# Second layer's weights rebuilt from four fp32 sums on every pass, a wider spread of the gate's products, and another order of the two layers on TensorE

## The chip, the cores and the metric

The kernel runs on one core of one Trainium2 chip. The metric is device time in microseconds (us), the median of several runs. The profile is of one execution: its rows count from the start of the span, the time from the first to the last instruction.

## What is computed

Pooled attention, then two feed-forward parts over 2304 tokens of width 512. The last part is the one that the change touches:

```python
logits = x @ w_gate
logits = logits - logits.max()
P = np.exp(logits)
for _ in range(8):
    P /= P.sum(1, keepdims=True) + 1e-09
    P /= P.sum(0, keepdims=True) + 1e-09
    P *= N / E
out = np.zeros((N, D), dtype=np.float32)
for e in range(E):
    h = np.maximum(x @ w1[e], 0.0)
    ye = h @ w2[e]
    out += P[:, e:e + 1] * ye
```

Here N = 2304, D = 512, E = 8, and the hidden width of each expert is 1024.

## The kernel before

Every fp32 operand of a product is kept as a pair, a rounded high part and the low rest, and each product is three matmuls (high by high, high by low, low by high). `split` (L93) makes a pair: ScalarE copies to the high part (`whi`), VectorE or GpSimd subtracts it from the source to give the low part (`wlo`).

Up to about 533 us the kernel does the attention and the first feed-forward part. Then it goes over three pairs of token blocks (768 tokens each) and, inside each pair, over 16 units (8 experts by two halves of the hidden width). One unit of one pair is a **step**, 48 in all. In a step TensorE does the first layer of that unit and, woven into it, the second layer of the unit before.

The first layer (`first_layer`, L740) is a Strassen-like scheme of seven products P1, P5, P6, P2, P7, P3, P4, for two halves g = 0 and 1 of the unit: 14 products of six matmuls of 384 columns, called **a0 to a13** here (a0 to a6 for g = 0, a7 to a13 for g = 1). P1 goes to the PSUM bank `px`, ScalarE copies it to `py`, and P6 adds to that copy. P5 and later P3 use the one bank `pv`. The results leave the banks through ScalarE (relu) and VectorE.

In pair 0 the second layer is plain (`plain_layer`, L843): six groups **L** of 24 matmuls of 256 columns, with the four blocks of the second weight matrix. In pairs 1 and 2 it is Strassen-like as well (`strassen_layer`, L860): three row groups 0, 1, 2, each with four parts of 12, 12, 12 and 6 matmuls of 256 columns. The strings `PLAIN`, `SWAP` (the step between pairs 0 and 1) and `STRASSEN` write out the order of TensorE by hand: `a` is the next product of the first layer, `L` the next plain group, a digit the next part of that row group. The other engines' orders are made by a scheduler; each engine, and SP's DMA queue, works strictly in its order. What follows a product is hung on its slot with `put(places, todo)`.

The second layer's weights: in pair 0 `w2_pieces` (L617) loads the fp32 weights of a unit, splits the four blocks, forms four sums on GpSimd (P5, P6, P7, P4), splits these too, and writes seven pairs to DRAM (`w2c`, 14 DMAs of 256 KB a step). In pairs 1 and 2 `w2_cached` (L667) loads the seven pairs, 14 DMAs a step. The first layer's weights go the same way (`w1_pieces` L574, `w1c`, `w1_cached`), loaded seven slots ahead.

The gate (softmax and eight rounds of row and column scaling, the "halves") is hung on the slots of the first steps by the list `rest` (L969): one entry after each even slot.

Of the kernel before, what the change touches and what calls it, by code (L numbers as in the profile page):

```python
# [58 lines left out]
def fused_kernel(ctx: ExitStack, tc: tile.TileContext, qT, kT, vT, v0, wa1, wb1, wa2, wb2, wg, out):  # L59
# [459 lines left out]
    def gate_max():  # L519

        sk, lg = gate["sk"], gate["lg"]
        m1 = sk.tile([P, 1], F32, tag="m1", name="m1")
        nc.vector.tensor_reduce(out=m1, in_=lg, op=ALU.max, axis=AX.XY)
# [90 lines left out]
    def w2_pool(name):  # L614
        return wp if name in ("P1", "P5") else gate["wp2"]

    def w2_pieces(u):  # L617

        src, w = {}, {}

        def load(h):
            src[h] = xp.tile([P, 2, DM], F32, tag=("xh5", "xl5")[h], name="raw2")
            nc.sync.dma_start(out=src[h], in_=wb2[u, :, h])

        def b(h, d):
            return src[h - 1][:, :, (d - 1) * HD:d * HD]

        def flat(t):
            return t.rearrange("p (g n) -> p g n", g=2)

        def cut(what, pool, lo_engine):
            hi = pool.tile([P, FU], F32R, tag="w", name="vhi")
            lo = pool.tile([P, FU], F32R, tag="w", name="vlo")
            nc.scalar.activation(out=flat(hi), in_=what, func=AF.Copy)
            lo_engine.tensor_tensor(out=flat(lo), in0=what, in1=flat(hi).bitcast(F32), op=ALU.subtract)  # L635
            return hi, lo

        def keep(name, parts):
            for k, part in enumerate(parts):
                nc.sync.dma_start(out=w2c[u, ORDER.index(name), k], in_=part.bitcast(F32))  # L640

        def block(h, d):
            w[h - 1, d - 1] = cut(b(h, d), gate["wp2"], nc.gpsimd)
            name = {(1, 1): "P1", (2, 1): "P2", (2, 2): "P3"}.get((h, d))
            if name:
                keep(name, w[h - 1, d - 1])

        def tmp():
            return gate["tmp"].tile([P, 2, HD], F32, tag="s", name="t")

        def total(name):
            if name == "P5":
                src["t"] = combine(tmp(), b(1, 2), b(1, 1), ALU.subtract)
                what = src["t"]
            elif name == "P6":
                what = combine(src["t"], b(2, 2), src["t"], ALU.subtract)
            elif name == "P7":
                what = combine(tmp(), b(2, 2), b(1, 2), ALU.subtract)
            else:
                what = combine(src["t"], b(2, 1), src["t"], ALU.subtract)  # L660
            keep(name, cut(what, gate["wp2"], nc.vector))

# [452 lines left out]
```

## Time and profile before

| | us |
|---|---|
| median of 3 runs (lowest, highest) | 2041.63 (2041.26, 2043.84) |
| the profiled execution's own time | 2042.21 |
| its span | 2040.5 |
| TensorE busy in the span | 1966.0 |
| VectorE, ScalarE, GpSimd busy | 1380.9, 992.3, 770.8 |

A matmul is pipelined: in the timeline its modelled end lies after the start of the next, so the rate is read from one start to the next, and busy time is no measure of it. An idle time in square brackets is followed by what ended it. The granted clock is the share of TensorE's full clock, 1.00 being 2.4 GHz and 0.50 being 1.2 GHz.

### The profile page before, as it was taken

The numbers are of one execution on the slowest core, as the hardware profiler recorded it, in microseconds if no ns is written. First come the engines' busy times: TensorE is split into PE (matmuls) and PEld (weight loads), VectorE is DVE, ScalarE is ACT, GpSimd is POOL, SyncE is SP. The second block draws the span as 40 slices with busy tenths as digits, with TensorE's granted clock in tenths as the row PEclk, the third lists the DMA queues.
The fourth block names the chain that finished last, engine by engine and source line by source line (L and its number), as shares of the span: only waits on it lengthen the run. The fifth ranks groups of instructions, "written<-read, shape, count | busy, mean of one in ns | idle before, by whom it ended". The sixth has DMA issues, their size and how long they took to land.

```text
span 2040.5 us, 36395 instructions
## 1 busy us (share of the span) xinstructions
PE 1966.0 (96%) x13220; PEld 1917.3 (94%) x13220; DVE 1380.9 (68%) x2279; ACT 992.3 (49%) x2133; POOL 770.8 (38%) x646
## 2 busy tenths in 40 slices
PE   6799999999889999999999999999999999999999
PEld 4689899999889999999999999999998999999999
DVE  8988776655786555556565676667667666666766
ACT  5676566655544444434443444444445444444443
POOL 7755644433344545454532221222223222222212
PEclk8899999999989999999999999999999999999999
DMA  7433331212688988888896776677677777667763
GB/s 254 144 123 126 113 119 53 84 52 77 228 292 296 304 276 301 270 293 292 278 316 222 266 263 229 240 275 250 225 256 250 241 261 275 230 235 269 258 230 121
DMA packets 257458, 453.32 MB, mean 222 GB/s; under 512 B 25568, under 2 KB 86752, under 8 KB 257280
## 3 DMA queue, kind: packets, MB, share of 16 engines
q1 hardware_dynamic: 257280, 451.01, 64.5%
q8 instruction: 104, 1.70, 0.3%
q14 instruction: 74, 0.61, 0.1%
HBM read 317.21 MB, written 133.69 MB: 221 GB/s over the span
## 4 chain that ended last, share of the span: by engine, by line
PE 76%; DVE 6%; DMA 6%; POOL 4%; ACT 3%; issue 3%; SPq 0%; ACTq 0%; POOLq 0%; DVEq 0%
PE pc L869 13%; PE py L736 13%; PE qc L869 10%; PE po L852 8%; PE px L736 8%; PE pv L736 8%; DMA w2c<-vhi 2%; PE ph L138 2%; PE po L137 2%; PE po L139 2%; PE ph L139 2%; PE po L138 2%; PE ph L137 2%; POOL vlo L635 1%; POOL t L571 1%
## 5 line engine op out<-in xcount | busy, mean ns | idle before, releaser
L869 PE MATMUL pc<-wc,gh 128*128 128x256 f32 x1536 | 284.1, 280 | 0.0
L571 POOL TENSOR_TENSOR sf<-spare 128x384 f32<-128x384 f32 x64 | 65.7, 1027 | 509.9 <-DVE spare L800 509.9
L869 PEld LDWEIGHTS pc<-wc,gh 128*128 128x128 f32 x1536 | 241.1, 188 | 0.0
L736 PE MATMUL py<-xc,wc 128*128 128x384 f32 x1152 | 236.1, 340 | 0.9 <-DVE c L794 0.6
L869 PE MATMUL pc<-wc,gl 128*128 128x256 f32 x768 | 215.6, 281 | 0.0
L869 PE MATMUL qc<-wc,gh 128*128 128x256 f32 x1152 | 214.1, 280 | 1.5 <-DVE pc L888 1.5
L736 PEld LDWEIGHTS py<-xc,wc 128*128 128x128 f32 x1152 | 196.6, 189 | 7.4 <-ACT py L751 5.1
L783 DVE TENSOR_TENSOR gl<-sf,gh 128x384 fp32r<-128x384 f32 x256 | 183.8, 758 | 10.8 <-ACT gh L782 7.3
L869 PEld LDWEIGHTS qc<-wc,gh 128*128 128x128 f32 x1152 | 185.9, 188 | 2.0 <-DVE pc L888 1.8
L869 PE MATMUL qc<-wc,gl 128*128 128x256 f32 x576 | 161.7, 281 | 0.0
L571 POOL TENSOR_TENSOR sf<-sf 128x384 f32<-128x384 f32 x64 | 80.8, 1262 | 210.9 <-DVE gl L783 210.9
L736 PE MATMUL pv<-xc,wc 128*128 128x384 f32 x768 | 156.2, 338 | 3.8 <-DVE xc L716 2.0
L736 PE MATMUL px<-xc,wc 128*128 128x384 f32 x768 | 154.3, 335 | 0.0
L852 PE MATMUL po<-vlo,gh 128*128 128x256 f32 x768 | 153.1, 281 | 0.0
L852 PE MATMUL po<-vhi,gl 128*128 128x256 f32 x768 | 152.8, 281 | 0.0
L852 PE MATMUL po<-vhi,gh 128*128 128x256 f32 x768 | 152.6, 281 | 0.0
L782 ACT ACTIVATE gh<-sf 128x384 fp32r<-128x384 f32 x256 | 119.9, 517 | 52.5 <-POOL sf L571 32.8
L869 PEld LDWEIGHTS pc<-wc,gl 128*128 128x128 f32 x768 | 145.1, 189 | 0.2 <-DVE gl L783 0.2
L137 PE MATMUL ph<-xh,whi 128*128 128x384 f32 x384 | 131.3, 346 | 5.9 <-DVE r L389 5.9
L736 PEld LDWEIGHTS pv<-xc,wc 128*128 128x128 f32 x768 | 131.0, 189 | 4.6 <-DVE xc L716 2.2
L138 PE MATMUL ph<-xl,whi 128*128 128x384 f32 x384 | 131.5, 343 | 0.7 <-DVE xl L370 0.7
L138 PE MATMUL po<-gl,whi 128*128 128x384 f32 x384 | 129.5, 338 | 0.8 <-POOL gl L392 0.8
(203 smaller groups left out, 5136.1 us busy)
## 6 DMA issues: line engine op xcount, KB each, us to landing
wc<-w1c SPq DMA_DIRECT2D x448, 256.0 KB, 5.2
wc<-w2c SPq DMA_DIRECT2D x448, 256.0 KB, 5.4
w1c<-whi SPq DMA_DIRECT2D x112, 256.0 KB, 3.4
w1c<-wlo SPq DMA_DIRECT2D x112, 256.0 KB, 3.3
w2c<-vhi SPq DMA_DIRECT2D x112, 256.0 KB, 3.9
w2c<-vlo SPq DMA_DIRECT2D x112, 256.0 KB, 4.3
raw<-wa SPq DMA_DIRECT2D x48, 512.0 KB, 6.2
raw<-wb SPq DMA_DIRECT2D x48, 512.0 KB, 4.6
```

Of the source, the lines that this page charges most:

```text
L137: nc.tensor.matmul(out=ps, lhsT=lh, rhs=rh, start=(i == 0), stop=False)
L138: nc.tensor.matmul(out=ps, lhsT=lh, rhs=rl, start=False, stop=False)
L139: nc.tensor.matmul(out=ps, lhsT=ll, rhs=rh, start=False, stop=(i == n - 1))
L571: nc.gpsimd.tensor_tensor(out=out, in0=x, in1=y, op=op)
L635: lo_engine.tensor_tensor(out=flat(lo), in0=what, in1=flat(hi).bitcast(F32), op=ALU.subtract)
L736: nc.tensor.matmul(out=ps, lhsT=l[:, k], rhs=r[:, c, :], start=(start and c + n == 0), stop=(c + n == 3), skip_group_check=True)
L782: nc.scalar.activation(out=hi, in_=t, func=AF.Copy)
L783: nc.vector.tensor_tensor(out=lo, in0=t, in1=hi.bitcast(F32), op=ALU.subtract)
L852: nc.tensor.matmul(out=po[:, d * HD:(d + 1) * HD], lhsT=l[:, r], rhs=w[f % 2, d][k][:, (f // 2) * HD:(f // 2 + 1) * HD], start=(f + n + d ...
L869: nc.tensor.matmul(out=ps, lhsT=l[:, r], rhs=m[:, k], start=(start and g + n == 0), stop=(g + n == 3), skip_group_check=True)
```

## The change

Second layer's weights. `w2_sums` loads a unit's raw weights once more, forms the four sums with GpSimd and writes them unsplit to DRAM (`w2s`, 4 DMAs of 256 KB); these jobs run in steps 2 to 14 of pair 0. `w2_piece` loads one fp32 tile of 256 KB (a block of the input, or a sum) into one of four buffers `st` and splits it: four blocks a step in pair 0, seven pieces a step in pairs 1 and 2. P2, P4 and the blocks (2,1), (2,2) take their low part on VectorE, all others on GpSimd. The write-out of 14 split tiles and the loads of 14 are gone.

Gate. `logits` and the maximum are cut in two, and `rest` names the slots: the last logits after a1 and a3, the maximum after a6, the exponential and first row scaling after a8, one half after a12 of step 0, then one after every odd slot of step 1.

Order. `PLAIN`, `STRASSEN` and the places of several `put` lists are new. The first unit's `w1_pieces` moves into the last task of the part before, the low parts of the first two units of the first layer go to GpSimd, and the inputs of pair 1 are prepared from slots 2 and 7 on.

```diff
+    w2s = dram.tile([NU, 4, P, FU], F32, name="w2s")
...
-            parts = split(what, nc.vector)
+            parts = split(what, nc.gpsimd if u < 2 else nc.vector)
...
+    W2RAW = {"P1": (1, 1), "P2": (2, 1), "P3": (2, 2)}
+    W2SUM = ("P5", "P6", "P7", "P4")
+
+    def w2_piece(u, name, w):
+
+        src = st.tile([P, FU], F32, tag="st", name="st")
+        if name in W2SUM:
+            nc.sync.dma_start(out=src, in_=w2s[u, W2SUM.index(name)])
+        else:
+            i, j = W2RAW.get(name, name)
+            nc.sync.dma_start(out=src, in_=wb2[u, :, i - 1, j - 1])
+        engine = nc.vector if name in ("P2", "P4") or name in BLOCKS[2:] else nc.gpsimd
+        w[name] = split(src, engine, wp if name == "P1" else gate["wp2"])
+
+    def w2_sums(u):
...
+        def total(k):
+            b = {(i, j): r[i - 1][:, j - 1, :] for i in (1, 2) for j in (1, 2)}
+            t, s = r[0][:, 2, :], r[1][:, 2, :]
+            out, x, y = ((t, b[1, 2], b[1, 1]), (s, b[2, 2], t), (b[1, 2], b[2, 2], b[1, 2]),
+                         (b[2, 1], b[2, 1], s))[k]
+            combine(out, x, y, ALU.subtract)
+            nc.sync.dma_start(out=w2s[u, k], in_=out)
...
+                    if f == 2 and j == GRP[1][1] and u == U1 - 1:
+                        w_op, w_load, w_todo = w1_pieces(0)
+                        run(w_load, 2)
...
-    gate["wp2"] = right(ctx, "wp2", 18, reuse_waits="tile")
+    gate["wp2"] = right(ctx, "wp2", 16, reuse_waits="tile")
+    st = right(ctx, "st", 4, reuse_waits="tile")
...
-    rest = [[lambda: logits(GRP[1][1])], [gate_max], [gate_exp, sinkhorn_rows], [], half, [], half]
-    rest += [half] * (SINKHORN_ITERS - 3) + [[sinkhorn_columns]]
+    rest = [{1: [late_logits], 3: [late_turn], 6: [max_turn], 8: [gate_exp, sinkhorn_rows], 12: half},
+            {2 * k + 1: half for k in range(SINKHORN_ITERS - 2)}]
+    rest[1][13] = half[:1]
...
-    GB = {"gl": 20, "gh": 16}
-    PLAIN = "aaLaaLaaLaaLaaLaaLaa"
+    GB = {"gl": 17, "gh": 17}
+    PLAIN = "aaLaaLaaLaaaLaaLaaLa"
     SWAP = "aaLaLLLLLsaaaaaaaaaaa"
-    STRASSEN = "aaa0a1a01a01a01a2aa2a2a2aa"
+    STRASSEN = "aa0a1a0a1a0a1a0a2a1a2a2a2a"
...
-                    put((0, 0), load)
-                    put((1, 3, 5, 7, 8, 9, 10, 11) if not last else (1, 2, 3, 4, 5, 6, 7, 8), todo)
-                    put(range(0, 14, 2), w_todo)
+                    put((2, 4, 6, 8), [lambda b=b, u=u, w=w2: w2_piece(u, b, w) for b in BLOCKS])
+                    put(range(5, 12), w_todo)
+                    if n > 1 and not last:
+                        for k in (0, 6)[:1 + (n > 11)]:
+                            put((k, k + 2, k + 3, k + 3, k + 4), w2_sums(jobs.pop(0)))
...
-                    put((6, 7, 8, 9, 10, 11, 12), [lambda m=m, u=u, w=w2: w2_cached(u, w, m) for m in ORDER])
+                    put(range(7, 14), [lambda m=m, u=u, w=w2: w2_piece(u, m, w) for m in ORDER])
...
-                    put((8, 8) if pair == 0 else (2, 2), x_load)
-                    put((10, 10, 11, 11, 12, 12, 13) if pair == 0 else range(7, 14), x_todo)
+                    put((2, 2), x_load)
+                    put(range(7, 14), x_todo)
```

**VectorE in step 0 of pair 0**, from the maximum's arrival (`nm`) to the first column sum (`cs`), which the gate's next product waits for. Before:

```order
L536 COPY nm<-pb 128x1
L725 SCALAR_TENSOR_TENSOR gl<-c_5757,gh 128x384
L543 TENSOR_REDUCE rw<-pr 128x18
L544 TENSOR_SCALAR rw<-rw 128x18
L545 RECIPROCAL rw<-rw 128x18
L725 SCALAR_TENSOR_TENSOR gl<-pv_5701,gh 128x384
L546 TENSOR_TENSOR pr<-pr,rw 128x144
L97 TENSOR_TENSOR wlo<-s,whi 128x512
L725 SCALAR_TENSOR_TENSOR gl<-py,gh 128x384
L548 TENSOR_REDUCE cs<-pr 128x8
```

With the change:

```order
L546 COPY nm<-pb 128x1
L738 TENSOR_TENSOR pv_5806<-py,s_5813 128x384
L553 TENSOR_REDUCE rw<-pr 128x18
L554 TENSOR_SCALAR rw<-rw 128x18
L555 RECIPROCAL rw<-rw 128x18
L556 TENSOR_TENSOR pr<-pr,rw 128x144
L707 SCALAR_TENSOR_TENSOR gl<-px_5790,gh 128x384
L558 TENSOR_REDUCE cs<-pr 128x8
```

The low part of a first-layer weight (L97) and two of the three `gl` rows have left this chain; one addition to `pv` came in.

**ScalarE in a step of pair 0**, up to P1's copy (`py`). `vhi` is the high part of a second-layer weight, `t` a sum just made, `whi<-raw` and `whi<-s` belong to the first layer, `gh` to its results, `st` is a fresh fp32 load. Before:

```order
L634 ACTIVATE vhi<-t 128x512
L724 ACTIVATE gh<-c_8549 128x384
L634 ACTIVATE vhi<-t 128x512
L724 ACTIVATE gh<-pv_8447 128x384
L724 ACTIVATE gh<-py 128x384
L634 ACTIVATE vhi<-t 128x512
L96 ACTIVATE whi<-raw 128x512
L751 ACTIVATE py<-px_8620 128x384
```

With the change:

```order
L706 ACTIVATE gh<-pv_9226 128x384
L96 ACTIVATE whi<-st 128x512
L96 ACTIVATE whi<-s 128x512
L96 ACTIVATE whi<-st 128x512 x2
L706 ACTIVATE gh<-py 128x384
L96 ACTIVATE whi<-st 128x512
L733 ACTIVATE py<-px_9398 128x384
```

The rows `vhi<-t`, whose tiles were also written out to `w2c`, are gone from ahead of `py`; the blocks' rows `whi<-st` stand there instead.

**ScalarE in the second half of a step of pair 2**, from P2's result (`spare`, after a10) to P1's copy of the next step. `c` is P7's result, `sf<-pv` P3's (it frees the bank `pv`), `sf<-py` P4's. Before:

```order
L802 ACTIVATE spare<-px_23205 128x384
L805 ACTIVATE gh<-px_23205 128x384
L802 ACTIVATE c_23315<-c_23315 128x384
L802 ACTIVATE sf<-pv_23237 128x384
L782 ACTIVATE gh<-spare 128x384
L782 ACTIVATE gh<-c_23315 128x384
L802 ACTIVATE sf<-py 128x384
L751 ACTIVATE py<-px_23385 128x384
```

With the change:

```order
L784 ACTIVATE spare<-px_23262 128x384
L787 ACTIVATE gh<-px_23262 128x384
L96 ACTIVATE whi<-st 128x512 x3
L784 ACTIVATE c_23380<-c_23380 128x384
L96 ACTIVATE whi<-st 128x512 x2
L784 ACTIVATE sf<-pv_23286 128x384
L764 ACTIVATE gh<-spare 128x384
L764 ACTIVATE gh<-c_23380 128x384
L96 ACTIVATE whi<-st 128x512
L784 ACTIVATE sf<-py 128x384
L733 ACTIVATE py<-px_23474 128x384
```

Six of the seven new splits (the seventh, P1's, stands further ahead) lie between these results: five ahead of `sf<-pv`, one ahead of `sf<-py`.

## Rows read from the trace of the kernel before

**Rows 1.** The page, busy time and share of the span of each engine.

```profile
PE 1966.0 (96%) x13220; PEld 1917.3 (94%) x13220; DVE 1380.9 (68%) x2279; ACT 992.3 (49%) x2133; POOL 770.8 (38%) x646
```

**Rows 2.** Stretch, us, busy PE PEld DVE ACT POOL, granted clock, DMA share, GB/s.

```profile
533.38:601.00 67.62, 52.42 (x308) 49.23 (x307) 52.55 (x111) 27.29 (x52) 32.43 (x24) 0.87 0.84 292
601.00:1062.00 461.00, 449.06 (x3231) 444.59 (x3230) 270.23 (x416) 197.51 (x376) 230.15 (x165) 1.00 0.86 290
...
1105.00:1530.00 425.00, 425.00 (x3030) 422.80 (x3029) 286.26 (x460) 192.32 (x458) 97.39 (x86) 1.00 0.70 245
1530.00:1560.00 30.00, 26.07 (x167) 24.83 (x166) 24.65 (x32) 17.55 (x36) 13.98 (x8) 0.94 0.71 236
```

**Rows 3.** TensorE's waits, 533 to 601 us: total, times, longest.

```profile
PE pc L555 <- DVE cs L548: 10.6, 4, 7.8
PE pv L736 <- DVE gl L725: 1.8, 1, 1.8
PE pm L525 <- DVE m L523: 1.6, 1, 1.6
```

**Rows 4.** Timeline of TensorE in that stretch: start, duration, then the instruction.

```profile
555.24 0.52 PE L736 MATMUL px<-xl,whi 128*128 128x384 f32 x1
555.56 0.52 PE L736 MATMUL px<-xh,wlo 128*128 128x384 f32 x1
...
570.49 0.59 PE L555 MATMUL pc<-cs,ones 128*128 128x8 f32 x2 [7.81 <-DVE cs L548]
```

**Rows 5.** Timeline of VectorE, then of GpSimd, 543 to 553 us.

```profile
544.29 0.15 DVE L536 COPY nm<-pb 128x1 f32<-128x1 f32 x1
...
549.79 1.77 DVE L97 TENSOR_TENSOR wlo<-s,whi 128x512 fp32r<-128x512 f32 x1
...
551.95 0.40 DVE L548 TENSOR_REDUCE cs<-pr 128x8 f32<-128x144 f32 x1
...
548.43 4.26 POOL L635 TENSOR_TENSOR vlo<-raw,vhi 128x512 fp32r<-128x512 f32 x3
```

**Rows 6.** Waits of TensorE and ScalarE, 601 to 1062 us, and ScalarE's timeline.

```profile
PE py L736 <- ACT py L751: 10.3, 11, 1.7
...
ACT vhi L634 <- DMA w2c<-vhi: 76.6, 34, 6.8
...
691.33 0.63 ACT L634 ACTIVATE vhi<-t 128x512 fp32r<-128x512 f32 x1 [4.22 <-DMA w2c<-vhi]
...
692.38 0.47 ACT L751 ACTIVATE py<-px 128x384 f32<-128x384 f32 x1
```

**Rows 7.** Timeline of TensorE in one step of pair 2.

```profile
1815.67 1.21 PE L736 MATMUL pv<-xc,wc 128*128 128x384 f32 x6
1816.71 1.32 PE L736 MATMUL py<-xc,wc 128*128 128x384 f32 x6
1817.87 0.40 PE L869 MATMUL pc<-wc,gh 128*128 128x256 f32 x2
...
1819.31 1.21 PE L736 MATMUL px<-xc,wc 128*128 128x384 f32 x6
```

**Rows 8.** Groups by line: busy us, mean ns, idle before and its releasers.

```profile
L96 ACT ACTIVATE whi<-raw 128x512 fp32r<-128x512 f32 x136 | 82.9, 625 | 27.9 <-DMA raw<-wb1f 8.7 <-DMA raw<-wa1f 7.0 <-PE po L139 6.8
...
L635 POOL TENSOR_TENSOR vlo<-raw,vhi 128x512 fp32r<-128x512 f32 x64 | 91.2, 1440 | 70.9 <-PE po L852 40.9 <-DMA w2c<-vlo 15.2 <-ACT vhi L634 9.1
...
L97 DVE TENSOR_TENSOR wlo<-raw,whi 128x512 fp32r<-128x512 f32 x80 | 60.5, 757 | 3.5 <-PE px L736 2.0 <-PE pv L736 0.2
```

**Rows 9.** DMA issues: KB each, median us to landing.

```profile
wc<-w2c SPq DMA_DIRECT2D x448, 256.0 KB, 5.4
...
raw<-wb1f SPq DMA_DIRECT2D x14, 512.0 KB, 3.6
out<-acc SPq DMA_DIRECT2D x18, 256.0 KB, 2.0
```

**Rows 10.** TensorE's longest wait, 1530 to 1560 us.

```profile
PE pv L736 <- ACT sf L802: 1.8, 1, 1.8
```

More of the change, by code (lines that the diff above doesn't have):

```diff
@@ L485, in open_gate @@
         gc = right(ctx, "gc", 1, reuse_waits="tile")
-        gate["sk"] = right(ctx, "sk", 2, reuse_waits="tile")
+        gate["sk"] = right(ctx, "sk", 1, reuse_waits="tile")
         gate["tmp"] = right(ctx, "tmp", 3, reuse_waits="tile")
@@ L504, in logits, with logits_first @@
     def logits(j):
-        sk = gate["sk"]
+        lt = logits_first(j)
+        logits_turn(j, lt)
+    def logits_first(j):
         ps = gate["ps"][0].tile([P, NB], F32, tag=gate["ps"][1], name="pl")
@@ L517, in logits, with max_first, max_turn @@
         nc.vector.tensor_copy(out=gate["lg"][:, j * TPB:(j + 1) * TPB, :], in_=pq)
[L519 to L523, printed above, removed]
+    def max_first():
+        gate["m1"] = gate["sk"].tile([P, 1], F32, tag="m1", name="m1")
+        nc.vector.tensor_reduce(out=gate["m1"], in_=gate["lg"], op=ALU.max, axis=AX.XY)
+    def max_turn():
         pm = gate["ps"][0].tile([P, P], F32, tag=gate["ps"][1], name="pm")
-        nc.tensor.transpose(pm[:1, :], m1, ident)
-        m2 = sk.tile([1, 1], F32, tag="m2", name="m2")
+        nc.tensor.transpose(pm[:1, :], gate["m1"], ident)
+        m2 = gate["sk"].tile([1, 1], F32, tag="m2", name="m2")
         nc.vector.tensor_reduce(out=m2, in_=pm[:1, :], op=ALU.max, axis=AX.X, negate=True)
@@ L612, in w1_cached @@
         return t[:, 0, :], t[:, 1, :]
[L614 to L661, printed above, removed]
-        todo = [lambda h=h, d=d: block(h, d) for h, d in ((1, 1), (1, 2), (2, 1), (2, 2))]
-        todo += [lambda n=n: total(n) for n in ("P5", "P6", "P7", "P4")]
-        return w, [lambda h=h: load(h) for h in range(2)], todo
@@ L667, in w2_cached @@
-    def w2_cached(u, w, name):
-        parts = []
-        for k in range(2):
-            t = w2_pool(name).tile([P, FU], F32R, tag="w", name="wc2")
-            nc.sync.dma_start(out=t.bitcast(F32), in_=w2c[u, ORDER.index(name), k])
-            parts.append(t)
-        w[name] = parts
+    W2RAW = {"P1": (1, 1), "P2": (2, 1), "P3": (2, 2)}
[9 more added lines that the diff above has]
+        w[name] = split(src, engine, wp if name == "P1" else gate["wp2"])
@@ new lines, in w2_sums, with load @@
+    def w2_sums(u):
+        r = {}
+        def load():
+            for i in range(2):
+                r[i] = xp.tile([P, 3, FU], F32, tag=("xh5", "xl5")[i], name="rw2")
+                nc.sync.dma_start(out=r[i][:, :2], in_=wb2[u, :, i])
+        def total(k):
[5 more added lines that the diff above has]
+            nc.sync.dma_start(out=w2s[u, k], in_=out)
+        return [load] + [lambda k=k: total(k) for k in range(4)]
@@ L943, in fused_kernel @@
     run(side, len(side))
-    w_op, w_load, w_todo = w1_pieces(0)
-    run(w_load, 2)
     run(w_todo, 3)
@@ L1029, in fused_kernel @@
                     x_next, x_load, x_todo = x_pieces(pair + 1)
-                    put((8, 8) if pair == 0 else (2, 2), x_load)
-                    put((10, 10, 11, 11, 12, 12, 13) if pair == 0 else range(7, 14), x_todo)
-                for k in range(0, 14, 2):
-                    if rest:
-                        after[k] += rest.pop(0)
+                    put((2, 2), x_load)
+                    put(range(7, 14), x_todo)
+                for k, todo in (rest.pop(0) if rest else {}).items():
+                    after[k] += todo
             else:
@@ L1055, in fused_kernel @@
                     gfirst.close()
[L1056 removed]
+                    gb = ctx.enter_context(tc.tile_pool(name="gb", bufs=17, reuse_waits="tile"))
                     spare = xp.tile([P, KC, NB], F32, tag="xl1", name="spare")
```

20 lines of the change are left out of this document (14 added, 6 removed).

## The prediction

> **What bounds the kernel now.** I read the page first: TensorE is busy in 96% of the span [rows 1], so all a change of order can win is the rest, plus what TensorE loses at half clock. The table by stretches says where that lies [rows 2]. From 1105 to 1530 us (pair 1) TensorE is busy for all of 425.00 us at a granted clock of 1.00: one step follows the other without a hole. In the first 67.62 us behind the first feed-forward part it is busy for 52.42 only, and the clock's mean is 0.87. From 601 to 1062 us (the rest of pair 0) 449.06 of 461.00 are busy. Between 1530 and 1560 us, where pair 2's inputs are made, 26.07 of 30.00 are. Then I read who is waited for in these stretches.
>
> At the start TensorE waits for the gate: 10.6 us in four waits for the column sums, one of them 7.81 long, 1.8 for a low part that VectorE makes late, 1.6 for the maximum [rows 3, 4]: 14.0 us. The chain from `nm` at 544.29 to the end of `cs` at 552.35 takes 8.1 us on VectorE, and a weight's low part of 1.77 us stands in it [rows 5].
>
> In the rest of pair 0 TensorE waits 11 times, 10.3 us in all, for ScalarE's copy of P1 [rows 6]. ScalarE is not busy then: it holds still for `w2c`, 76.6 us in 34 waits. The two rows of its timeline show the link: `vhi` stood 4.22 us for a write-out to give its tile free, began at 691.33, and only then, at 692.38, came the copy [rows 6].
>
> **The change, part by part.** The sum is made against the profiled execution's 2042.21 us, which lies 0.6 us above the median of the runs.
>
> *Gate.* The pieces now stand further apart. The longest chain has a12's slot instead of a8's: four products, a9 to a12, lie between the exponential and the column sum's product. A product's six matmuls go by in 1.04 us (1815.67 to 1816.71) [rows 7], so they cover 4.2 us. The chain itself loses the 1.77 us row and some smaller ones and gains an addition to `pv`: 8.1 less some 2.3 is 5.8. A wait of 1.6 stays there. In step 1 each half has two products and an L before the next, as it had before when the waits were short (10.6 less 7.81 leaves 2.8 for three); I leave 2.4 us for the six of them. The maximum has three products in front instead of two: nothing left. The 1.8 us for a low part stays at a third, 0.6, since VectorE has less to do there. So 14.0 becomes 4.6, a gain of 9.4. At half clock a matmul of 384 columns starts 0.32 us after the last (555.24 to 555.56) [rows 4], against 0.174 at full clock (1.04 by six). The clock fell twice, each time behind such waits; a mean of 0.87 over 67.62 us is 17.6 us at half rate, of which some 8 were idle anyway; the other 9.6 cost 4.8. If no wait over 2 us stays, most of this comes back: 4.5. Together **14 us**; bounds 6 and 18.
>
> *Pair 0.* `w2c` is no longer written, so what ScalarE stood for is gone, and I expect 8.5 of the 10.3 us back. A modelled matmul ends about 0.17 us after its successor's start (duration 0.34, rate 0.174), so each of the 11 waits is that much longer than listed: 1.8 more. **10 us**. Bounds: 2, if loads into `st` hold ScalarE as the write-outs did, and 12. GpSimd forms the sums as before, four a step (eight in steps 12 to 14), and splits two tiles fewer; the 4 DMAs of 256 KB for the sums and 1 MB more of loads take the place of 14 writes, so SP's queue gets shorter.
>
> *Pairs 1 and 2, work added.* Seven splits a step: seven on ScalarE at 0.63, two on VectorE at 0.76, five on GpSimd at 1.44 [rows 8]. A step lasts some 29.6 us (14 products at 1.04, 126 second-layer matmuls at a twelfth of 1.44) [rows 7]; the shares of pair 1 [rows 2] give it 13.4 us of ScalarE, 19.9 of VectorE, 6.8 of GpSimd. They go to 17.8, 21.4 and 14.0. None becomes the bound by its sum. What can cost is the order. ScalarE's splits wait for their loads, and behind them stands `sf<-pv`, which frees the bank for P5 (a1) of the next step. There are four `st` tiles, so P3's load goes out only when P5's split is finished on GpSimd. Count from the end of a10: two copies of P2's result on ScalarE, about 1.0; P5's high part 0.63; its low part on GpSimd 1.44; the load's landing; P3's high part 0.63; the copy that frees `pv`, 0.47 as the like copy in [rows 6]: 4.2 plus the landing. TensorE meanwhile has a11, a12, a13 and a0 at 1.04 each, and parts of 12, 12 and 6 matmuls at 1.44 (1817.87 to 1819.31) [rows 7] and half that: 7.8. So the landing may take **3.6 us** before TensorE stands. The landings of the trace go from 2.0 us for a lone write of 256 KB, through 3.6 for 512 KB read in a quiet stretch, to 5.4 for the `w2c` loads [rows 9]. These last come in bursts of up to three loads per slot at a DMA share of 0.70 [rows 2]; the change takes seven of 28 loads of a step away and spreads the rest. I take 3.2, nearest the quiet read of twice the size, so nothing on average, and 0.1 us a step for scatter: 3 us in 31 steps. Bounds: 0, and at 5.4 us 1.8 a step, 56 in all.
>
> *Pairs 1 and 2, order.* P6 of g = 0 comes two products after P1 and waits for its copy: 1.16 us to the next row instead of 1.04 [rows 7]. This repeats in all 31 steps of the two pairs: 3.5 us. `STRASSEN` now puts a part of row group 0 between, so this goes. It pays for the scatter: together **0**.
>
> *Between the pairs.* Between 1530 and 1560 us 3.9 us are idle and the clock's mean is 0.94, 1.8 us more [rows 2]. The longest wait is for `sf<-pv`, behind ScalarE's splits of the new inputs [rows 10]. The seven weight splits now fall on the same slots: 4.4 us more for ScalarE, of which the wider order of parts hides most. I take **1 us worse**; bounds 3 better and 6 worse. Before pair 1 the inputs are now prepared eight slots earlier, but in `SWAP` eleven products run with nothing between and ScalarE has the splits on top; I take 0, between 3 better and 4 worse.
>
> *First part's end.* The first unit's split now runs beside the last task there, on GpSimd, which is busy for half of the gate's stretch [rows 2]. It gives VectorE room, and I count 0.
>
> Sum: 14 + 10 + 0 - 1 = 23 us. 2042.21 less 23 is 2019.2; with the 0.6 us to the median I say **2018.5 us**.
>
> **Rivals.** *The landing decides (slower).* As worked out, each us of landing over 3.6 costs 31 us: each step waits for P3's tile, ScalarE stands, `pv` is not free. From 4.4 us on the gain is gone; at 5.0 the time is 2018.5 + 1.4 by 31, that is 2062. For it speaks the 5.4 of [rows 9]; against it, that DMA falls to three quarters. *GpSimd against VectorE.* In the stretch of [rows 5] GpSimd ran three splits without a break, and VectorE's split took 1.77 us against a mean of 0.76 [rows 8]. Five splits a step on GpSimd may each hold back a VectorE row with two SBUF inputs; at 1 us each that is 5 us a step, VectorE then at 26.4 of 29.6, and pieces come late. At 0.4 us a step it costs 12: 2030. The Trainium skill, SBUF — State Buffer, section "SBUF: two separate sides", says that GpSimd and a VectorE instruction with two SBUF inputs take a shared port pair by an exclusive lock and that the other blocks fully; the trace agrees (1.77 against 0.76). *A wait returns in pair 0.* ScalarE stands for `st` loads instead of write-outs: 8 of the 10 us stay lost, 2026. *All of it.* The upper bounds for gate and pair 0, P6's 3.5 us, and 3 us at each change of pair: 18 + 12 + 3.5 + 6 is 39.5, or 2002.
>
> **How the numbers follow.** The forecast (2012 to 2024) has 0.45, the full gain 0.13, the two partial losses together (2024 to 2036) 0.25, the landing 0.13, and 0.04 is left for a stall at the first part's end. I take 2004 to 2041 as the range: it leaves out about 0.04 below and 0.13 above. A measurement of this kernel tells 0.2%, 4 us, from no change: faster means below 2037.5. From the cases: faster 0.82, same 0.06, slower 0.12.
>
> **What would show it.** Right: no `vhi` or `w2c` among ScalarE's waits from 601 to 1062 us and under 2 us for P1's copy; under 5 us for the column sums and a clock near 1.00 in the gate's stretch; steps some 0.1 us shorter than before in pairs 1 and 2 with no TensorE wait; DMA's share there near 0.5. Wrong: steps 0.3 us longer than before or more, with ScalarE's `whi` waiting for `st` and TensorE waiting for `sf` or `py`; or GpSimd's rows above 1.8 us with VectorE late.

## The result, and the profile after

The changed kernel takes 2060.12 us (median of 4 runs, 2057.43 to 2062.24), the kernel before 2042.25 (4 runs): ratio 1.0086, 95% interval 1.0069 to 1.0104. It is slower by 0.9%, above the range of the forecast (2018.5; 2004 to 2041). Its profiled execution took 2057.43 us, with a span of 2055.7.

Cutting both spans at the first `px` matmul of a0 shows where the time went. Step n is the n-th of the 48, counted from 0; a step in which TensorE waits for nothing lasts as long as its matmuls.

| stretch | before, us | changed, us | difference | forecast |
|---|---|---|---|---|
| start to step 0 | 533.38 | 531.13 | -2.25 | with the gate |
| steps 0 and 1 (gate) | 73.01 | 64.23 | -8.78 | -14 |
| steps 2 to 8 | 229.52 | 234.80 | +5.28 | -10 up to step 15 |
| steps 9 to 15 | 226.38 | 220.06 | -6.32 | |
| step 16 (into pair 1) | 36.79 | 40.80 | +4.01 | 0 |
| steps 17 to 30 | 413.78 | 423.36 | +9.58 | 0 with 33 to 46 |
| steps 31 and 32 (into pair 2) | 65.40 | 69.70 | +4.30 | +1 |
| steps 33 to 46 | 413.67 | 423.43 | +9.76 | |
| step 47 to the end | 48.57 | 48.19 | -0.38 | 0 |

The rows of the table by stretches of the changed kernel, cut at these steps (columns as in [rows 2]):

```profile
531.13:595.36 64.23, 55.85 (x346) 52.43 (x345) 49.46 (x109) 27.10 (x52) 38.88 (x30) 0.95 0.90 302
595.36:830.16 234.80, 224.75 (x1599) 222.31 (x1598) 138.76 (x198) 80.84 (x159) 133.54 (x97) 0.99 0.86 291
830.16:1050.22 220.06, 220.06 (x1597) 219.91 (x1597) 127.00 (x182) 82.00 (x159) 60.59 (x41) 1.00 0.58 187
1050.22:1091.02 40.80, 36.05 (x230) 34.03 (x229) 23.60 (x30) 14.39 (x30) 17.51 (x11) 0.92 0.67 224
1091.02:1514.38 423.36, 418.44 (x2942) 412.94 (x2941) 319.60 (x477) 239.21 (x544) 191.07 (x153) 1.00 0.57 181
```

Three things stand in them. In pair 1 TensorE has holes for the first time: 418.44 busy of 423.36, where [rows 2] had 425.00 of 425.00; the clock there is 1.00, so it is waiting and nothing else. In steps 9 to 15 there is no hole left, as forecast. In steps 2 to 8 the DMA runs at 291 GB/s, after that at 187, though the source spreads the sums over steps 2 to 14.

The page of the changed kernel, first the busy times, then the chain that ended last by engine and by line, then two groups:

```profile
PE 1974.6 (96%) x13220; PEld 1921.2 (93%) x13220; DVE 1461.8 (71%) x2297; ACT 1071.6 (52%) x2293; POOL 973.8 (47%) x788
...
PE 40%; DMA 5%; ACT 1%; POOL 1%; DVE 1%; issue 0%; SPq 0%; POOLq 0%; ACTq 0%
PE pc L851 12%; PE py L718 9%; PE qc L851 8%; PE pv L718 5%; PE px L718 5%; DMA st<-w2s 5%; PE po L834 1%; ACT whi L96 1%; POOL wlo L97 1%; ACT sf L784 0%; DVE gl L765 0%; SPq L621 0%; POOL sf L581 0%; DVE xc L698 0%; POOL x1r L695 0%
...
L96 ACT ACTIVATE whi<-st 128x512 fp32r<-128x512 f32 x288 | 174.8, 628 | 125.5 <-DMA st<-w2s 41.1
...
L718 PEld LDWEIGHTS pv<-xc,wc 128*128 128x128 f32 x768 | 129.6, 189 | 18.5 <-ACT sf L784 18.2
```

GpSimd rose from 38 to 47% [rows 1]. The load of a sum (`st<-w2s`) makes up 5% of the chain that ended last; in the kernel before DMA had 6% of it, of which 2% were the write-outs `w2c`. ScalarE's splits stood 41.1 us for that load, and TensorE's products into `pv` (P5) stood for `sf`, the copy that frees `pv`. In pair 1 alone, the waits of TensorE and of ScalarE (1105 to 1512 us):

```profile
PE pv L718 <- ACT sf L784: 4.5, 10, 0.6
...
ACT whi L96 <- DMA st<-w2s: 18.9, 15, 1.7
```

One step's end shows the link. Timelines of ScalarE, GpSimd, SP's queue, VectorE and TensorE around the change from step 22 to step 23, whose a0 starts at 1272.21:

```profile
1266.51 1.17 ACT L96 ACTIVATE whi<-st 128x512 fp32r<-128x512 f32 x2
...
1272.73 0.63 ACT L96 ACTIVATE whi<-st 128x512 fp32r<-128x512 f32 x1 [1.46 <-DMA st<-w2s]
1273.27 0.47 ACT L784 ACTIVATE sf<-pv 128x384 f32<-128x384 f32 x1
...
1267.22 2.55 POOL L97 TENSOR_TENSOR wlo<-st,whi 128x512 fp32r<-128x512 f32 x2 [2.86 <-ACT whi L96]
...
1268.60 1.51 SPq L631 DMA_DIRECT2D st<-w2s  x2
...
1270.90 0.54 DVE L782 SCALAR_TENSOR_TENSOR spare<-pv,c 128x384 f32<-128x384 f32 x1
...
1272.21 1.21 PE L718 MATMUL px<-xc,wc 128*128 128x384 f32 x6
1273.80 1.31 PE L718 MATMUL pv<-xc,wc 128*128 128x384 f32 x6 [0.38 <-ACT sf L784]
```

Read it backwards. TensorE's P5 began at 1273.80, when `sf<-pv` (from 1273.27) was done. That copy could have begun at 1271.44, when VectorE was through with `pv`. It did not, because a split stood in front of it in ScalarE's order, and that split waited 1.46 us for its source. The source's load was issued at 1268.60, as soon as GpSimd had finished the first of two low parts (1267.22, 2.55 us for both), and landed 4.1 us later. In the mean of steps 17 to 30 P5 starts 1.49 us after a0 starts, where six matmuls take 1.04: this one wait is 0.45 us a step.

In steps 2 to 8, waits of TensorE (595 to 1056 us; after step 8 next to none), a wait of SP's queue (595 to 740 us), then one of TensorE's waits on SP, GpSimd, ScalarE and TensorE:

```profile
PE py L718 <- ACT py L733: 3.8, 3, 1.5
PE po L834 <- ACT gh L706: 3.5, 3, 1.8
PE po L834 <- DVE gl L707: 3.2, 4, 1.6
...
SPq L653 <- POOL rw L581: 24.0, 17, 4.5
```

```profile
656.78 0.60 SPq L590 DMA_DIRECT2D raw<-wa  x1
...
663.24 1.28 POOL L581 TENSOR_TENSOR s<-raw 128x512 f32<-128x512 f32 x1 [8.41 <-DMA raw<-wa]
...
664.55 0.63 ACT L96 ACTIVATE whi<-s 128x512 fp32r<-128x512 f32 x1 [4.49 <-POOL s L581]
665.09 0.47 ACT L706 ACTIVATE gh<-py 128x384 fp32r<-128x384 f32 x1
...
665.62 0.50 PE L834 MATMUL po<-whi,gh 128*128 128x256 f32 x2 [1.49 <-ACT gh L706]
```

The waits for the copy of P1 fell from 10.3 us [rows 6] to 3.8, but 6.7 us of waits of the plain groups L for `gh` and `gl` are new. In the case shown a load of w1, issued at 656.78 and landed 6.4 us later, keeps GpSimd waiting; a split on ScalarE waits for GpSimd, and the result's `gh` stands behind that split. Over the 145 us of its line SP's queue stood 24.0 us for the sums that GpSimd makes (`rw`) before it could store them.

Into pair 2 (step 31), the longest wait on TensorE, and what VectorE did ahead of the sum that it waits for:

```profile
1545.32 0.58 PE L851 MATMUL qc<-whi,gh 128*128 128x256 f32 x1 [5.14 <-DVE pc L870]
```

```profile
1542.37 2.55 DVE L698 TENSOR_TENSOR xc<-x1r,xc 128x768 fp32r<-128x768 f32 x1
1544.85 0.42 DVE L870 TENSOR_TENSOR pc<-qc,t 128x256 f32<-128x256 f32 x1
```

VectorE is through its queue without a pause; a low part of pair 2's x stands in front of the sum.

### The profile page after: what moved, and what is told of

Read it like the earlier page. It is cut to its first block, busy times and chain, and to the rows that moved or that the text cites. A ratio compares the mean times of both kernels' runs of the same rounds, so it can differ in the third digit from the quotient of the medians.

```text
span 2055.7 us, 36446 instructions
## 1 busy us (share of the span) xinstructions
PE 1974.6 (96%) x13220; PEld 1921.2 (93%) x13220; DVE 1461.8 (71%) x2297; ACT 1071.6 (52%) x2293; POOL 973.8 (47%) x788
## 5 line engine op out<-in xcount | busy, mean ns | idle before, releaser
L97 POOL TENSOR_TENSOR wlo<-st,whi 128x512 fp32r<-128x512 f32 x192 | 275.7, 1452 | 152.3 <-ACT whi L96 106.0
L96 ACT ACTIVATE whi<-st 128x512 fp32r<-128x512 f32 x288 | 174.8, 628 | 125.5 <-DMA st<-w2s 41.1
L851 PE MATMUL pc<-whi,gl 128*128 128x256 f32 x768 | 215.0, 280 | 1.2 <-DVE gl L765 1.2
L851 PE MATMUL pc<-whi,gh 128*128 128x256 f32 x768 | 215.3, 280 | 0.0
L851 PE MATMUL pc<-wlo,gh 128*128 128x256 f32 x768 | 214.9, 280 | 0.0
L581 POOL TENSOR_TENSOR sf<-spare 128x384 f32<-128x384 f32 x64 | 66.7, 1042 | 227.4 <-DVE spare L782 227.4
L851 PE MATMUL qc<-whi,gh 128*128 128x256 f32 x576 | 160.9, 279 | 5.1 <-DVE pc L870 5.1
L851 PE MATMUL qc<-whi,gl 128*128 128x256 f32 x576 | 162.4, 282 | 0.0
L851 PE MATMUL qc<-wlo,gh 128*128 128x256 f32 x576 | 161.8, 281 | 0.0
L834 PE MATMUL po<-whi,gh 128*128 128x256 f32 x768 | 154.2, 283 | 3.5 <-ACT gh L706 3.5
L834 PE MATMUL po<-whi,gl 128*128 128x256 f32 x768 | 153.7, 282 | 3.2 <-DVE gl L707 3.2
L97 POOL TENSOR_TENSOR wlo<-raw,whi 128x512 fp32r<-128x512 f32 x66 | 90.3, 1383 | 119.0 <-PE po L138 36.3
```

The costliest lines, as they stand in the source:

```text
L96: nc.scalar.activation(out=hi, in_=src, func=AF.Copy)
L97: lo_engine.tensor_tensor(out=lo, in0=src, in1=hi.bitcast(F32), op=ALU.subtract)
L581: nc.gpsimd.tensor_tensor(out=out, in0=x, in1=y, op=op)
L834: nc.tensor.matmul(out=po[:, d * HD:(d + 1) * HD], lhsT=l[:, r], rhs=w[f % 2 + 1, d + 1][k][:, (f // 2) * HD:(f // 2 + 1) * HD], start=(f ...
L851: nc.tensor.matmul(out=ps, lhsT=l[:, r], rhs=m[:, k], start=(start and g + n == 0), stop=(g + n == 3), skip_group_check=True)
```

## The experiments

The kernel before was run beside each of them and took 2039.7 to 2043.3 us (medians), so times of different experiments compare to some 3 us.

Theory A: in pairs 1 and 2 the source's load decides, through ScalarE's order. Theory B: GpSimd's low parts stretch VectorE's rows, and that makes `sf` late. In the first text for A I called the waiting piece P3, freed by P5's low part; by the program's order of ScalarE and SP it is P5 of the step after, in the tile that GpSimd's low part of P7 frees. The kind of chain is the same. So the splits that the rows of the two orders show ahead of the first `sf` are P7, P3, P4 and then P1 and P5 of the step after, with its P6 ahead of the second; the one further ahead is P2, not P1.

**Six source buffers.**

```
-        src = st.tile([P, FU], F32, tag="st", name="st")
+        if extra and name in EXTRA:    # {"P6": "xh5", "P3": "xl5"}
+            src = xp.tile([P, FU], F32, tag=EXTRA[name], name="sx")
+        else:
+            src = st.tile([P, FU], F32, tag="st", name="st")
```

The two further buffers are idle in pairs 1 and 2 except in step 31, where they hold the next x; there the four of before are used.

> Changed kernel, but in pairs 1 and 2 the fp32 sources of P6 and P3 have two further buffers of their own, so P3's load no longer waits for GpSimd's low part of P5 of the same step; GpSimd's low parts stay as they are. Theory A (the source load: P3's load starts only when GpSimd has finished P5's low part, lands 3.8 us later, ScalarE stands in order at that split and holds the copy that frees pv, about 0.7 us a step): the steps of pairs 1 and 2 go from 30.25 back to 29.6 us, 28 x 0.65 = 18 us off, about 2042 us (2038 to 2046), and the wait of ScalarE for st falls from 18.9 us in pair 1 to under 4. Theory B (GpSimd's low parts lengthen VectorE's subtractions, gl<-sf 939 ns for 758, so that the copy from pv is late): the wait goes from ScalarE's load to VectorE's result, steps stay over 30.0 us, time 2054 to 2060.

Measured: 2031.73 us (4 runs; before 2041.1 on the same chip, ratio 0.9954, interval 0.9937 to 0.9970). Pair 1's steps by the same cut, and ScalarE's wait for sums there:

```profile
1048.39:1083.69 35.30, 33.27 (x230) 31.39 (x229) 22.61 (x30) 14.71 (x30) 17.11 (x11) 1.00 0.70 227
1083.69:1496.19 412.50, 412.50 (x2942) 412.40 (x2941) 318.88 (x477) 240.56 (x545) 187.73 (x154) 1.00 0.60 188
```

```profile
ACT whi L96 <- DMA st<-w2s: 1.4, 1, 1.4
```

14 steps take 412.50 us, 29.46 each, without a hole: 10.9 less than in the changed kernel, and 10.8 less in steps 33 to 46. The arithmetic, ScalarE's splits and GpSimd's low parts are all still there. P5 starts 1.04 us after a0 again: of the 0.78 us a step that came back, 0.45 stood in front of P5, and the rest, some 0.3, lay between the next four products. A is right, and this version is 0.5% faster than the kernel before. It gained 10 us more than expected; by the profiles 3.7 more in these 28 steps, 5.5 in step 16 and 3.4 in steps 2 to 8, which are written alike in the two. Six other runs with steps 2 to 8 written so took 228.3 to 239.3 us there, so most of the 3.4 is chance, and a difference of a few us in these steps tells nothing.

**All low parts on VectorE.** Edit: `engine = nc.gpsimd if name in BLOCKS[:2] else nc.vector`.

> Changed kernel, but all low parts of pairs 1 and 2 are VectorE's, none GpSimd's; buffers as they are. Theory B (contention): gl<-sf falls back to some 758 ns, the waits on pv go, 2038 to 2044 us. Theory A (source load): P5's low part takes 0.75 us on VectorE for 1.28 on GpSimd, so P3's load starts at most 0.5 us earlier and a wait of 0.2 to 0.5 us a step stays: 2046 to 2056 us, with ScalarE still waiting for st.

Measured: 2084.72 us. VectorE's groups in pair 1, of the kernel before, of the changed kernel and of this one:

```profile
L783 DVE TENSOR_TENSOR gl<-sf,gh 128x384 fp32r<-128x384 f32 x104 | 74.5, 757 | 3.8 <-ACT gh L782 2.3
...
L783 DVE TENSOR_TENSOR gl<-c,gh 128x384 fp32r<-128x384 f32 x26 | 25.0, 962 | 16.7 <-ACT gh L782 16.7
```

```profile
L765 DVE TENSOR_TENSOR gl<-sf,gh 128x384 fp32r<-128x384 f32 x104 | 95.6, 959 | 22.7 <-PE pc L851 16.2 <-ACT gh L764 6.5
...
L765 DVE TENSOR_TENSOR gl<-c,gh 128x384 fp32r<-128x384 f32 x25 | 24.3, 974 | 0.0
```

```profile
L765 DVE TENSOR_TENSOR gl<-sf,gh 128x384 fp32r<-128x384 f32 x100 | 71.4, 754 | 16.2 <-PE pc L851 16.2
...
L765 DVE TENSOR_TENSOR gl<-c,gh 128x384 fp32r<-128x384 f32 x25 | 13.7, 547 | 0.0
```

B has the row `gl<-sf` right (757 ns before, 959 with GpSimd's splits, 754 without them) and the time wrong: without the splits on GpSimd the kernel is 25 us slower still, though VectorE also has more to do there. The row `gl<-c` says nothing on the splits: it took 962 ns in the kernel before too, which makes none in pair 1. Half of these rows stand beside one of GpSimd's sums of the first layer's results (`sf<-spare`) and take 1.37 us, the others 0.55 or 0.56, before and after alike; in this run no `gl<-c` has a GpSimd instruction beside it. ScalarE's waits for `st` stay (20.7 us), and TensorE also waits 7.8 us for P1's copy; why VectorE's fuller queue costs that much I did not trace. A had expected 2046 to 2056, so its size was wrong here too.

**The order of before in pairs 1 and 2.** Edit: `STRASSEN = "aaa0a1a01a01a01a2aa2a2a2aa"`.

> Changed kernel with the order of pairs 1 and 2 on TensorE of the kernel before. There row group 2's second part comes one product earlier against the next step's P5 (six products behind it instead of five), so that the chain that ends in P3's split has 1.05 us more. Theory A (source load): the waits on pv go and P6's 0.12 us a step come back: 28 x (0.7 - 0.12) = 16 us off, about 2044 us (2040 to 2050). Theory B (contention): GpSimd and VectorE do the same work, nothing is gained, 2056 to 2064 us.

Measured: 2133.93 us, both expectations wrong. A step's end on ScalarE and on TensorE:

```profile
1255.57 1.30 ACT L96 ACTIVATE whi<-st 128x512 fp32r<-128x512 f32 x2 [3.94 <-DMA st<-w2s]
1256.78 0.51 ACT L784 ACTIVATE c<-c 128x384 f32<-128x384 f32 x1
...
1258.45 1.66 PE L718 MATMUL pv<-xc,wc 128*128 128x384 f32 x6 [1.95 <-ACT sf L784]
```

The chain is A's, and longer. Here the scheduler put the waiting split in front of `c<-c` as well, which VectorE needs before it lets `pv` go, so load, `c`, VectorE's row and `sf` follow one after the other. Counting TensorE's products after a part, as I did, says nothing while the scheduler chooses what stands in front of what on ScalarE.

**Before, with the gate spread and both new orders.** Edit: `rest`, its helpers, `PLAIN` and `STRASSEN` of the change; everything on w2 as before.

> Kernel before (w2 parts cached as they were) with only the gate's products spread and the two new orders on TensorE. By the prediction's terms: gate -12 (without the earlier w1 load), pair 0 between -2 and +4 since the sums stay where they were, order of pairs 1 and 2 -3.5: about 2027 us (2024 to 2033). If the spread gives back its gain in pair 0 as the changed kernel's steps 2 to 7 did (5.8 us), 2033 to 2038.

Measured: 2052.36 us, slower than before (ratio 1.0053, interval 1.0038 to 1.0068) and outside both ranges. Steps 2 to 15 took 474.5 us where the kernel before has 455.9; steps 17 to 30 took 412.7 where it has 413.8, which is what the new order of pairs 1 and 2 is worth by itself.

**Before, with the gate spread alone.**

> Kernel before with only the gate's products spread; w2 parts, both orders on TensorE and buffers as before. The kernel with spread and both orders took 4.8 us off step 0 and 1.5 off step 1, and lost 18.6 us in steps 2 to 15. If the new order of pair 0 costs that loss, it goes here: 2041 - 6 = 2035 us (2033 to 2038). If the spread pushes work into pair 0 and costs it, steps 2 to 15 stay long: 2045 to 2056 us.

Measured: 2040.10 us (ratio 0.9984, interval 0.9974 to 0.9994), between the two ranges; steps 2 to 15 took 454.1 us. So the loss of the run before, 20 us in these steps, is the new plain order's. The spread gave 2.8 us only; what TensorE waits for in its gate stretch:

```profile
PE pc L565 <- DVE cs L558: 10.5, 4, 4.0
```

Before it was 10.6 [rows 3]. The 7.81 is gone, the sum is not.

**Six buffers, pair 0 in the order of before.** Edit: `PLAIN = "aaLaaLaaLaaLaaLaaLaa"`.

> Changed kernel with six source buffers in pairs 1 and 2 (2031.7 us), and pair 0's order on TensorE of the kernel before. Theory O (the new order brings TensorE's plain groups onto ScalarE's and VectorE's last halves of the step before, 6.7 us of waits for gh and gl in steps 2 to 5): those waits go, steps 2 to 8 shorten by 3 to 6 us, 2026 to 2029 us. Theory Q (late w1 loads and GpSimd's sums hold ScalarE's queue, whatever TensorE's order): the waits turn into waits on ScalarE's copy of P1, 2030 to 2036 us.

Measured: 2040.47 us, both expectations wrong: 8.7 us slower than with the new order, 7.8 by the ratios to the kernel before (0.9992 and 0.9954). The waits of L for `gh` and `gl` are gone, as O has it, but in steps 2 to 14 products into `pv` wait 10.2 us, 12 times, for `gl`. Steps 9 to 14 take 32.4 us each instead of 31.4, step 16 41.2. Over steps 2 to 15 the new order costs 20 us with the cached parts and saves 7 with the sums (2.8 to 7.5 against the single six-buffer runs that have it): what is right for TensorE depends on what else stands in ScalarE's and VectorE's orders.

**Six buffers, sums written late.** Edit: `if n > 6 and not last: for k in (0, 6):`.

> Changed kernel with six source buffers in pairs 1 and 2 (2031.7 us), and the sums of w2 made in steps 7 to 14, two units a step, none in steps 2 to 6. Theory Q (late loads and GpSimd's sums): steps 2 to 6, 165.2 us together in the kernel with six buffers, fall to near 5 x 31.45 = 157.3, 6 to 8 us off; steps 7 to 11 gain some of it back as waits, 2 to 6 us; about 2028 us (2025 to 2033). Theory O (the order): steps 2 to 6 stay within 2 us of 165.2.

Measured: 2033.15 us, steps 2 to 6 168.0 us. The run tells nothing on Q, since the sums did not move. DMA issues of one step (step 4, or nearly; KB each and median us to landing), changed kernel and this one:

```profile
w2s<-rw SPq DMA_DIRECT2D x8, 256.0 KB, 2.5
raw<-wa SPq DMA_DIRECT2D x2, 512.0 KB, 6.5
```

```profile
w2s<-rw SPq DMA_DIRECT2D x8, 256.0 KB, 2.3
raw<-wa SPq DMA_DIRECT2D x2, 512.0 KB, 6.1
```

Eight stores in a step are two units' sums. Both kernels store all 64 sums in steps 0 to 8, 8 of them in steps 0 and 1 and 8 in each step from 2 on: their engines' orders are the scheduler's, and it lets work run ahead as soon as its data and buffers allow, wherever `put` hung it.

**Six buffers, sums tied to their step.** Edit: the sums' loads are queued on SP behind the last load of a block that is written ahead of them.

```
+                with behind("sp"):
+                    nc.sync.dma_start(out=r[i][:, :2], in_=wb2[u, :, i])
```

> Changed kernel with six source buffers in pairs 1 and 2 (2031.7 us), and in pair 0 the loads of w2's sums queued on SP behind the same step's loads of w2's parts. In the traces so far the sums run ahead of the place where they are written: 8 stores of w2s in each of steps 2 to 8 and next to none after, with the DMA at 280 to 306 GB/s in those steps and 180 to 187 from step 10 on, also in the kernel that was written to make none in steps 2 to 6. Theory H (the sums, run ahead, fill DMA and GpSimd in steps 2 to 8 and hold up w1's loads): now 4 stores a step, steps 2 to 8 fall from 231.4 us to 220 to 224, steps 9 to 14 stay within 3 us of 188.4, and 6 to 11 us go: 2021 to 2026 us. Theory O (TensorE's order alone): steps 2 to 8 stay over 229, 2030 to 2034 us.

Measured: 2043.92 us. Now 4 stores go out in step 4, at 251 GB/s instead of 293 in the changed kernel, and steps 2 to 8 take 223.6 us instead of 231.4 (228.3 to 239.3 in the runs that leave the sums free), as H expected. But steps 12 to 14, to which the source gives two units each, take 40.8, 35.3 and 34.3. By the trace the stores still run ahead: 8 in steps 11 and 12, 4 in step 13 and none in step 14, so two units in the step itself do not explain the last two.

**The same, two units only in steps 4 and 9.** Edit: `if n > 0 and not last: for k in (0, 6)[:1 + (n in (4, 9))]:`.

> The kernel with tied sums, but with one unit's sums in each of steps 1 to 14 and a second unit's only in steps 4 and 9, where it had two in each of steps 12 to 14. With tied sums the steps with one unit took 31.4 to 33.1 us and those with two 34.3 to 40.8. Theory H (where SP must issue two units' stores of sums, each store waiting for GpSimd, w1's loads behind them come late and ScalarE's splits of w1 hold its copies for TensorE): steps 12 to 14 fall from 110.4 to 94 to 97 us, steps 4 and 9 rise by 2 to 6 us each, the rest stays: 2026 to 2034 us. If something else in the tie costs those steps (the loads' place on SP), 2038 to 2046 us.

Measured: 2048.06 us. Steps 4 and 9 took 38.9 and 38.1 us, as H would have it, but steps 12 and 13 with one unit took 33.9 and 38.2, which H does not explain. Steps 2 to 8 of the run before show that fewer sums a step make these steps shorter; whether it is w1's loads, SP's queue or GpSimd that has less to bear is not shown, nor that the tie can be had without a price. Left free, the sums cost least of what I tried.

**Six buffers, the old order in step 31 alone.**

> Changed kernel with six source buffers in pairs 1 and 2 (2031.7 us), and in pair 1's last step alone the order on TensorE of the kernel before. Steps 31 and 32 took 69.9 us there and 65.4 in the kernel before, with 5.1 us in which TensorE waits for VectorE's sum behind the low parts of x. If the order puts row group 2's parts behind those low parts, 3 to 5 us go, about 2027.5 us. If the w2 parts that are split in that step are what fills VectorE and ScalarE, little goes, 2030 to 2034 us.

Measured: 2033.73 us, steps 31 and 32 71.6 us: no gain, so the new order is not what lengthens them.

**Tied sums, and x's low parts queued behind the second layer's sums in step 31.** The edit also moves the pieces of x in that step from slots 7 to 13 to slots 7, 8, 11, 11, 11, 12 and 13.

> The kernel of the run with tied sums, and in pair 1's last step the low parts of the next pair's x queued on VectorE behind the second layer's sums of the parts already written. If TensorE's 5.1 us wait there is VectorE's order (sum behind a 2.55 us low part of x), steps 31 and 32 go from 69.9 to 66 to 68 us, 2 to 4 us less than with tied sums alone. If those low parts are only late somewhere else (the next step's products wait for x), within 1 us of the run with tied sums.

Measured: 2044.42 us, steps 31 and 32 69.9 us, against 69.1 with tied sums alone. The wait for the sum fell from 5.1 to 2.7 us, and another took its place further on:

```profile
1551.67 2.29 PE L725 MATMUL pv<-xc,wc 128*128 128x384 f32 x6 [4.68 <-ACT sf L791]
```

**Six buffers, no splits of w2 in step 31.**

> Changed kernel with six source buffers in pairs 1 and 2 (2031.7 us), which leaves out the loads and splits of w2 in pair 1's last step alone; the step after uses the parts of the unit before, so that its second layer is not that of the reference. Theory W (these seven splits, three low parts on VectorE and four on GpSimd beside x's seven low parts, hold VectorE's sum that TensorE waits 5.1 us for): steps 31 and 32 go from 69.9 to 65.5 to 67 us, 2027.5 to 2029.5 us. If x's low parts alone do it, they stay over 69 us.

Measured: 2028.24 us; steps 31 and 32 take 64.4 us instead of 69.9. The seven splits and their loads, taken together, are what the change lost between the pairs. TensorE still waits there, 3.9 us for the same sum, with only x's low parts left beside it.

**Six buffers, w1's first low parts on VectorE; six buffers, the first w1 load late.** Edits: `split(what, nc.vector)`; and `w_load` back behind `run(side, len(side))`.

> Changed kernel with six source buffers in pairs 1 and 2 (2031.7 us), but w1's low parts of the first two units on VectorE as in the kernel before. Theory V (the gate's column sums wait for VectorE's queue, and what shortened steps 0 and 1 is that GpSimd took these low parts, not the spread, since the spread alone left 10.5 us of waits for cs where the kernel before had 10.6): waits for cs go from 5.3 back to 8 or more, steps 0 and 1 (64.7 us) take 3 to 7 us longer, 2034.5 to 2039 us. Theory S (the spread did it): within 1.5 us of 64.7, 2030 to 2033 us.

> Changed kernel with six source buffers in pairs 1 and 2 (2031.7 us), with the first w1 unit's load back at the end of the first part, as in the kernel before. If the earlier load made the first steps shorter, step 2 begins 2 to 6 us later than the 597.1 us there, 2034 to 2038 us. If it did nothing (the rest being the four splits in place of eight cuts and eight stores of w2 a step), within 1.5 us of 597.1 and 2030 to 2033 us.

Measured: 2032.64 and 2032.65 us. In the first the waits for `cs` rose to 8.9 us as theory V has it, yet steps 0 and 1 took 64.8 us (64.7 with six buffers): TensorE was busy for 54.4 us of them at a mean clock of 0.97, against 56.9 at 0.92, which gave back most of what the waits took. In the second step 2 began at 597.1, as with six buffers. Taken back by itself, neither part lengthens the start. Two earlier runs bound the rest. Steps 0 and 1 took 73.0 us before, 70.8 with the spread alone and 66.7 with the spread and both orders, where w2 still has its eight cuts and 14 stores a step; the changed kernel takes 64.2. So some 2.5 us are left for w2's four splits, and most of the gain came without them. Why the run with both orders is 4 us shorter there than the one with the spread alone is open; step 0 has the same order on TensorE in both, and a mean clock of 1.00 against 0.86.

## Why the prediction was wrong

- **Pairs 1 and 2, work added: the step that failed.** I counted 7.8 us of TensorE against 4.2 plus the load's landing, took 3.2 for the landing and wrote "nothing on average". The mechanism was right: GpSimd's low part, load, split, `sf`, P5. The landing was mis-sized: 4.1 us in the step shown, 3.8 as the page's median for the sums. The trace of before had 3.6 for a read of twice the size at rest and 5.4 for loads under load [rows 9], and I took a value below both. Nor does a step give back what another loses: the shortest of the changed kernel takes 29.51 us, so scatter only adds. By the prediction's sum a landing of 4.1 us costs 0.5 a step (15.5 in 31), and P5 was 0.45 late in the mean. Measured against six buffers the loss was 21.7 us over steps 17 to 30 and 33 to 46, 0.78 a step: the products behind P5 are late as well, which was in no term. Against the kernel before these steps lost 19.3 us, half of the 38 between the forecast and the sum of the table. The rival "the landing decides" gave 2062 at 5.0 us, close to 2060 by luck: less landing, and less gain elsewhere. The misnamed piece does not change the sum, since P7's low part on GpSimd and P5's load stand where P5's and P3's were counted; the forecast for the old order, which was built on the name, missed by 90 us.
- **Order of pairs 1 and 2: right in kind.** With the waits gone a step takes 29.46 us against 29.55, 2.3 us over these 28 steps; the new order alone in the kernel before gave 2.0. The forecast was 3.5 in 31.
- **Gate: 14 forecast, 11.0 measured up to step 2, for a wrong reason.** I set the chain from `nm` to the first `cs` against the wait of 7.81 us, and the two do not belong together. The first column sum's product waited 1.80 us. The 7.81 stand at 570.49 [rows 4], in step 1, at the third column sum, with low parts of w2 and three `gl` rows among the gate's pieces on VectorE:

```profile
552.41 0.60 PE L555 MATMUL pc<-cs,ones 128*128 128x8 f32 x2 [1.80 <-DVE cs L548]
...
565.40 1.71 DVE L635 TENSOR_TENSOR vlo<-t,vhi 128x512 fp32r<-128x512 f32 x1
...
570.02 0.41 DVE L548 TENSOR_REDUCE cs<-pr 128x8 f32<-128x144 f32 x1
```

  Nor did the spread give the first column sum more cover: four products, a5 to a8, lay between the exponential and its product before, and four, a9 to a12, do now. In the changed kernel the waits for `cs` fell to 5.3 us and the mean clock over steps 0 and 1 rose from 0.88 to 0.95, but the spread alone left 10.5 of 10.6 us. I had counted TensorE's products between the pieces and not VectorE's order, which is where the pieces are made. Waits in the changed kernel:

```profile
PE pc L565 <- DVE cs L558: 5.3, 6, 1.5
PE pv L718 <- DVE gl L707: 3.0, 1, 3.0
```

- **Pair 0: 10 forecast, 1.0 measured.** Steps 9 to 15 gave 6.3 us by themselves and have no wait left. In steps 2 to 8 the sums run ahead, two units a step, and these steps took 5.3 us longer. "the 4 DMAs of 256 KB for the sums and 1 MB more of loads take the place of 14 writes, so SP's queue gets shorter" is the sentence that fell: in those steps there are 8 stores, SP's queue stands for GpSimd before them, and w1's loads are in the same queue. That the sums are what costs is supported by the run with tied sums; which of the queue, the transfers and GpSimd does it stays open. The new order's part in it (3 to 8 us one way here, 20 the other in the kernel before) was in no term.
- **Between the pairs: 1 and 0 forecast, 4.3 and 4.0 measured**, the first within its bound of 6, the second at its bound of 4. With six buffers step 16 took 35.3 to 37.0 us in the runs that kept the new plain order, so the `st` loads were part of it.
- **GpSimd against VectorE** was in the traces and not in the time. `gl<-sf` went from 757 to 959 ns; with six buffers it is still at 861, and no product of pair 1 waits for VectorE.
- **The chances.** 0.82 for faster rested on a term of 0 whose own bounds went to 56. With those bounds the landing deserved far more than 0.13.

## What to carry to other kernels

A buffer that is refilled in the same step in which a slow engine frees it puts that engine's time plus a whole landing into the chain; count the buffers from the landing under the kernel's own load, and take the pessimistic row. On an engine with a strict order ask which copy for TensorE stands behind the instruction that may wait, and read that order from the built program rather than from the places in the source: the scheduler moves ready work ahead. An order on TensorE is tuned to the other engines' queues and has to be tuned again with every change to them.

## What the runs showed of the hardware

The same load of 256 KB lands later under more traffic. DMA issues of pair 1, from the changed kernel (184 GB/s there), then from the kernel of before with new orders (249 GB/s):

```profile
wc<-w1c SPq DMA_DIRECT2D x181, 256.0 KB, 3.2
st<-w2s SPq DMA_DIRECT2D x52, 256.0 KB, 3.7
```

```profile
wc<-w2c SPq DMA_DIRECT2D x185, 256.0 KB, 5.3
wc<-w1c SPq DMA_DIRECT2D x183, 256.0 KB, 4.2
```

`wc<-w1c` is the same transfer in both: 3.2 and 4.2 us. The Trainium skill, DMA: Bandwidth & Descriptors, section "Latency and other measured facts", says that a transfer's fixed cost is mostly the memory's round trip and is smaller when the memory is less loaded; the traces agree in direction. Whether the memory or the transfers ahead on the same queue make the difference, no run here separates.

VectorE's subtraction of two SBUF tiles (`gl<-c`, 128x384) took 0.56 us with no GpSimd instruction beside it and 1.37 beside `sf<-spare` on GpSimd in pair 1 of the kernel before (13 rows of each), 0.55 and 1.37 in the changed one. The Trainium skill, SBUF — State Buffer, section "SBUF: two separate sides", says that GpSimd and a VectorE instruction with two SBUF inputs take a shared port pair by an exclusive lock; the rows agree (1.37 against 0.56). The run without GpSimd's splits shows that such stretched rows can be the cheaper choice.
